# Cached attention for one token: straight-line engine programs become loops, with one place for keys and one for values

## The chip, the core and the metric

The kernel runs on one core of a Trainium2 chip. The core has a tensor engine (PE, whose weight loads the profile lists apart as PEld), a vector engine (DVE), a scalar engine (ACT), a general engine (POOL), a synchronising engine (SP) that issues most of the transfers here, and 16 DMA engines that move the data. All arrays lie in HBM at the start; the working memory on the chip is SBUF, and matrix products land in PSUM. The metric is the device time of one execution in microseconds, lower is better.

## What is computed

One new token `x` of 512 numbers passes two branches whose sums are added to it: attention over a cache of 65,536 keys and values, and a small two-layer network.

```python
def _A_ref(x, k_cache, v_cache, wq, wo):          # 32 query heads, 8 key heads, 128 wide
    q = (x @ wq).reshape(B, Sq, Hq, Dh).transpose(0, 2, 1, 3)
    k = jnp.repeat(k_cache, rep, axis=1)          # rep = 4 query heads share one key head
    v = jnp.repeat(v_cache, rep, axis=1)
    scores = jnp.einsum("bhqd,bhkd->bhqk", q, k) * (Dh ** -0.5)
    p = _softmax(scores, axis=-1)
    o = jnp.einsum("bhqk,bhkd->bhqd", p, v)
    return o.transpose(0, 2, 1, 3).reshape(B, Sq, Hq * Dh) @ wo

def _B_ref(x, w1, w2):
    return jnp.maximum(x @ w1, 0) @ w2            # 512 -> 1792 -> 512

xn = _layernorm(x)
out = x + _A_ref(xn, k_cache, v_cache, wq, wo) + _B_ref(xn, w1, w2)
```

All numbers are float32. Keys and values are 8 heads x 65,536 x 128, so 256 MB each (in units of 1,048,576 bytes); the weights `wq` and `wo` are 8 MB each, `w1` and `w2` 3.5 MB each. Every byte is read once.

## The kernel before

All engine programs are written out in full: the Python loops run when the kernel is built, so that each engine gets one long straight list of instructions. A framework of tiles sets the semaphores between them.

Keys and values come in chunks of 8 MB, four of keys and then four of values for each of the 8 heads (`load_k`, L85, and `load_v`, L94). They go through `ring`, a pool of three equal slots of 64 KB per partition, in the order in which they are used; `wq`, the two weights of the network and `wo` take their turns in the same three slots. SP issues all these loads in one queue and waits before each until the slot that it takes has been read to the end by PE. So up to three loads are under way or waiting to be read at any time.

For a chunk of keys (`score_chunk`) PE makes eight tiles `pt` of scores. A tile is four products (L179) that use 32 columns of PE each, and three buffers of PSUM take turns. DVE transposes each tile in blocks of 32x32 (L184), so that keys lie along partitions, and ACT copies the four useful columns of each block into `scores` (L186), which holds all scores of the head: 512 for each of the four query heads on each partition. After each chunk DVE takes a maximum (L187).

After the four chunks of a head, `softmax` forms the maximum over the whole head: a maximum on DVE (L195), a transpose on PE (L197), a maximum and a scaled diagonal on DVE (L199, L201), a product that hands it to all partitions (L203), a copy (L205), and four exponentials on ACT over 512 elements each (L207), which also sum up. Then, for each chunk of values, `value_chunk` makes 32 products (L218) that add up in `acc_o` over the whole head. `totals` and `output` form the sums and the normalised result of the head, the latter in the middle of the next head's scores. The network's product runs after head 0 (L154, L165, L250). After the last head `wo` is read in six loads (L318, L325), its rows are multiplied as they come in (L250, L265), and the result is added to `x` (L336) and written (L337).

[...] And the order of SP's queue is the order of use: keys of a head, values of that head, keys of the next.

## Time and profile before

| | |
|---|---|
| time, median of 3 runs | 1312.26 us (1312.25 to 1312.28) |
| the profiled execution's own time | 1312.33 us |
| its span, first to last instruction | 1310.6 us |
| moved by DMA | 561.65 MB, mean 429 GB/s |
| PE busy with matmuls | 639.9 us, 4460 records |
| DVE, ACT, POOL busy | 242.7, 103.6 and 0.7 us |
| mean clock granted to PE | 0.73 |

The span leaves out 1.7 us of the execution's time before and after the instructions. Busy time is no time on the path: an engine can be busy half of the time and never be waited for. In a row of a group, the part behind the `|` gives the busy time and the mean ns of one, and then the idle time of that engine just before these instructions with what ended it. In a row of the timeline the first number is the start in us from the begin of the span, the second the length, and the text in brackets the idle time before it.

### The profile page before, as it was taken

To read this page: it belongs to the slowest core of one execution; us is meant where nothing else is said; L and a number is where in the kernel's file an instruction comes from. 1 tells how busy PE (TensorE), PEld (TensorE's weight loads), DVE (VectorE), ACT (ScalarE), POOL (GpSimd) and SP (SyncE) were. 2 spreads that over 40 slices of the span, in tenths; PEclk is the share of its full clock that TensorE was granted. 3 is DMA by queue.
4 is the path that set the end of the run, shared out by engine and by line. 5 is a ranking of instruction groups with operands and counts; after the bars stand their busy time and mean duration, and the time that the engine had idled before them with its cause. 6 is when DMAs were issued, how large, how long until landed. Compare 5 with 4: busy or idle time off the path is not lost.

```text
span 1310.6 us, 10141 instructions
## 1 busy us (share of the span) xinstructions
PE 639.9 (49%) x4460; PEld 166.5 (13%) x4460; DVE 242.7 (19%) x408; ACT 103.6 (8%) x323; POOL 0.7 (0%) x6
## 2 busy tenths in 40 slices
PE   4345354545435544644544543644444563463455
PEld 1011011111111100111111110111111110011111
DVE  2242002230024200422003400233002420032200
ACT  0012000020001200101001110002000120010100
POOL 0000000000000000000000000000000000000000
PEclk9677687677777767767667767777866866776778
DMA  9999999999999999999999999999999999999997
GB/s 416 417 443 423 442 423 438 427 435 441 423 441 427 437 432 433 431 441 419 447 418 443 433 431 435 427 439 423 441 424 441 427 435 433 429 445 428 435 417 313
DMA packets 12428, 561.65 MB, mean 429 GB/s; under 512 B 1368, under 2 KB 1376, under 8 KB 1760
## 3 DMA queue, kind: packets, MB, share of 16 engines
q1 hardware_dynamic: 12240, 561.00, 99.3%
q8 instruction: 35, 0.57, 0.2%
q14 instruction: 9, 0.07, 0.0%
q10 hardware_dynamic: 144, 0.00, 0.0%
HBM read 560.99 MB, written 0.00 MB: 428 GB/s over the span
## 4 chain that ended last, share of the span: by engine, by line
DMA 77%; PE 19%; another core or an unknown queue 3%; ACT 0%; DVE 0%; issue 0%; SPq 0%; DVEq 0%; ACTq 0%
DMA slot<-k 44%; DMA slot<-v 30%; PE pt L179 9%; PE acc_o L218 8%; DMA slot<-wo 3%; PE acc_z L250 1%; ACT scores L207 0%; PE acc_y L265 0%; DVE chunk_max L187 0%; SPq L100 0%; DVE tr L184 0%; DVE z L256 0%; PE pm L203 0%; PE pm L228 0%
## 5 line engine op out<-in xcount | busy, mean ns | idle before, releaser
L179 PE MATMUL pt<-slot,qall 128*32 128x512 f32 x2048 | 295.4, 741 | 314.7 <-DMA slot<-k 314.7
L218 PE MATMUL acc_o<-slot,scores 128*16 128x512 f32 x2048 | 292.1, 734 | 249.3 <-DMA slot<-v 249.3
L184 DVE STREAM_TRANSPOSE tr<-pt 128x512 f32<-128x512 f32 x256 | 183.5, 717 | 829.5 <-PE pt L179 807.1
L186 ACT COPY scores<-tr 128x64 f32<-128x64 f32 x256 | 62.4, 244 | 1094.8 <-DVE tr L184 1094.8
L179 PEld LDWEIGHTS pt<-slot,qall 128*32 128x32 f32 x2048 | 80.7, 133 | 523.2 <-issue 472.5
L218 PEld LDWEIGHTS acc_o<-slot,scores 128*16 128x16 f32 x2048 | 61.4, 113 | 472.2 <-DMA slot<-v 273.6
L207 ACT ACTIVATE scores<-scores,bias 128x512 f32<-128x512 f32 x32 | 37.7, 1179 | 21.1 <-DVE bias L205 21.1
L187 DVE TENSOR_REDUCE chunk_max<-scores 128x4 f32<-128x512 f32 x32 | 33.5, 1047 | 7.7 <-ACT scores L186 7.7
L228 PE MATMUL pm<-part_sum,ones 128*128 128x4 f32 x16 | 4.7, 364 | 42.4 <-ACT scores L207 42.4
L154 PE MATMUL pm<-slot,xn 128*1 128x512 f32 (+1 forms) x96 | 14.7, 752 | 11.1 <-DMA slot<-wq 11.1
L240 DVE COPY o<-acc_o 128x512 f32<-128x512 f32 x8 | 5.3, 657 | 63.2 <-PE acc_o L218 63.2
L243 PE MATMUL pm<-norm,o 128*128 128x4 f32 x64 | 8.5, 257 | 11.2 <-DVE o L240 11.2
L160 DVE TENSOR_SCALAR rows<-pm 128x512 f32<-128x512 f32 x1 | 0.7, 691 | 70.0 <-PE pm L154 70.0
L197 PE MATMUL pm<-ident,m 128*4 128x128 f32 x8 | 2.3, 287 | 19.8 <-DVE m L195 19.8
L243 PEld LDWEIGHTS pm<-norm,o 128*128 128x128 f32 x64 | 7.8, 192 | 19.3 <-DVE o L240 19.3
L230 DVE RECIPROCAL r<-pm 128x4 f32<-128x4 f32 x8 | 1.5, 183 | 45.2 <-PE pm L228 45.2
L250 PE MATMUL acc_z<-slot,oT 128*1 128x512 f32 x48 | 7.3, 770 | 4.7 <-DMA slot<-wo 4.7
L228 PEld LDWEIGHTS pm<-part_sum,ones 128*128 128x128 f32 x16 | 4.0, 310 | 43.1 <-ACT scores L207 43.1
L250 PE MATMUL acc_z<-slot,hT 128*1 128x512 f32 x28 | 6.3, 996 | 2.5 <-DMA slot<-w 2.5
L203 PE MATMUL pm<-dg,ones 4*128 4x4 f32 x16 | 3.6, 296 | 5.0 <-DVE dg L201 5.0
L207 ACT ACTIVATION_READ_ACCUMULATOR scores<-scores,bias 128x1 f32 x32 | 6.0, 186 | 0.0
L154 PEld LDWEIGHTS pm<-slot,xn 128*1 128x1 f32 x96 | 2.8, 99 | 20.9 <-issue 20.6
(56 smaller groups left out, 38.6 us busy)
## 6 DMA issues: line engine op xcount, KB each, us to landing
slot<-wq SPq DMA_DIRECT2D x2, 4096.0 KB, 17.2
slot<-w SPq DMA_DIRECT2D x2, 3584.0 KB, 42.6
slot<-v SPq DMA_DIRECT2D x1, 4096.0 KB, 39.9
slot<-v SPq DMA_DIRECT2D x2, 2048.0 KB, 44.4
slot<-wo SPq DMA_DIRECT2D x1, 4096.0 KB, 41.7
slot<-wo SPq DMA_DIRECT2D x1, 2048.0 KB, 46.2
slot<-wo SPq DMA_DIRECT2D x1, 1024.0 KB, 48.1
slot<-k SPq DMA_DIRECT2D x32, 48.7
```

The costliest lines, as they stand in the source:

```text
L154: nc.tensor.matmul(pr[32 * c : 32 * c + 1, :n], xn[:, a : a + 1], weights(c, a), start=(a == 0), stop=(a == A - 1),)
L179: nc.tensor.matmul(pt[32 * c : 32 * c + 32, :], qall[:, h, :], t[:, lo : lo + TW], start=True, stop=True,)
L184: nc.vector.transpose(tr.rearrange("p b i -> p (b i)"), pt)
L186: nc.scalar.copy(scores[:, b0 : b0 + SUB, :], tr[:, :, :G])
L187: nc.vector.reduce_max(chunk_max[:, :, n], scores[:, n * NB : (n + 1) * NB, :].rearrange("p b g -> p g b"), axis=AX.X,)
L203: nc.tensor.matmul(pb[:, :G], ones[:G, :], dg, start=True, stop=True)
L207: nc.scalar.activation(scores[:, :, g], scores[:, :, g], AF.Exp, bias=bias[:, g : g + 1], scale=scale, accum_out=part_sum[:, g : g + 1],)
L218: nc.tensor.matmul(acc_o[32 * c : 32 * c + WIDE * G, :], scores[:, b : b + WIDE, :].rearrange("p b g -> p (b g)"), t[:, i * 512 : (i + 1) ...
L228: nc.tensor.matmul(pm[:, :G], ones, part_sum, start=True, stop=True)
L240: nc.vector.tensor_copy(o.rearrange("p b d -> p (b d)"), acc_o)
L243: nc.tensor.matmul(pm[:, :G], o[:, b, :], norm[:, b, :], start=(b == 0), stop=(b == WIDE - 1))
L250: nc.tensor.matmul(acc_z[32 * c : 32 * c + 1, :], lhsT, row, start=c not in begun, stop=last)
```

## The change

Each engine gets its own program with its own semaphores, inside one critical section that the framework of tiles does not order. PE, DVE and ACT run hardware loops: PE's body is one part of a head and runs 40 times, the bodies of DVE and ACT are a whole head and run 8 times. SP's and POOL's programs are still written out.

A head is cut into five parts of 7, 7, 6, 6 and 6 tiles (a tile is 2,048 keys, 1 MB), in place of four chunks of eight. For each part its keys and then its values are loaded, in turns, each into one place of its own (`ks`, `vs`, 56 KB per partition). The keys of the next part are issued once DVE has transposed the last tile of this part (`k_free`), the values of the next part once DVE has added this part's products to the sum (`v_free`). PE and DVE always work through seven tiles, also in parts of six; the weights of the seventh are then zero.

The maximum is taken per part, as a running one (`m`), and each part has its own bias. The exponentials are taken straight from the transposed tiles, part by part; ACT's copy of the scores is gone. The products of a part's values add up in `acc_o`, and DVE then forms `acc = alpha * acc + acc_o`, with `alpha` made by ACT from the two biases. At the end of a head DVE corrects the parts' sums and hands both to POOL, which keeps them (`fins`); normalisation is done once, after the last head. The rows of keys and values that are loaded lie 256 KB apart in HBM (64 KB before). The network's weights are loaded and used after the last head, ahead of `wo`, which goes to the place where `wq` was.

```diff
-CHUNK = 16384
+CHUNK = SK
+PART = [7, 7, 6, 6, 6]
+MOST = max(PART)
+NP = len(PART)
+STEPS = HKV * NP
...
-    ring = ctx.enter_context(tc.tile_pool(name="ring", bufs=3))
+    ks = place("ks", MOST * KEYS)
+    vs = place("vs", MOST * KEYS)
+    big = place("big", HKV * 2048)
+    tr = place("tr", MOST * SUB, 32)
+    wt = place("wt", MOST * SUB, G)
...
+        for i in range(STEPS):
+            h, n = divmod(i, NP)
+            lo, nt = sum(PART[:n]), PART[n]
+            src = v[h].rearrange("(p t b) d -> p t (b d)", p=P, b=SUB)[:, lo : lo + nt, :]
+            if i:
+                sy.wait_ge(k_free, i)
+            sy.dma_start(ks[:, : nt * KEYS], k[h, 0, :, lo * KEYS : (lo + nt) * KEYS]).then_inc(k_in, 16)
+            if i:
+                sy.wait_ge(v_free, i)
+            sy.dma_start(vs[:, : nt * KEYS], src.rearrange("p t f -> p (t f)")).then_inc(v_in, 16)
+        sy.wait_ge(k_free, STEPS)
...
+        w1_in = load(sy, "w1_in", t1, w1.rearrange("p a f -> p (a f)"))
+        w2_in = load(sy, "w2_in", t2, w2.rearrange("p j n -> p (j n)"))
...
+        with nc.Fori(0, STEPS, engines=[ENG.PE], head_slot={ENG.PE: 0}):
+            te.wait_ge(k_in, 16).then_inc(k_in, -16)
+            te.wait_ge(q_in, 1).then_inc(q_in, -1)
+            for s in range(MOST):
+                pt = (pa, pb)[s // 2 % 2][:, s % 2, :]
+                for c in range(CT):
+                    at = (s * CT + c) * TW
+                    i = te.matmul(pt[32 * c : 32 * c + 32, :], qcur, ks[:, at : at + TW], start=True, stop=True)
+                    if c == 0 and s in (4, 6):
+                        i._wait_ge(s_dve, s // 2 - 1)
+                if s % 2 or s == MOST - 1:
+                    i.then_inc(s_tiles, 1)
+            te.transpose(pm[:G, :P], m, ident)._wait_ge(s_dve, 3).then_inc(s_max, 1)
+            te.matmul(pm[:, P : P + G], ones[:G, :], dg[:, :G], start=True, stop=True)._wait_ge(s_dve, 4)
+            te.matmul(
+                pm[:, P + G : P + G + 1], rowg, dg[:, G : G + 1], start=True, stop=True
+            ).then_inc(s_max, 1)
+            te.sem_inc(s_dve, -4)
+            te.wait_ge(v_in, 16).then_inc(v_in, -16)
+            te.wait_ge(s_w, 1).then_inc(s_w, -1)
+            n = MOST * SUB // WIDE
+            for i in range(n):
+                c = i % CT
+                mm = te.matmul(
+                    acc_o[32 * c : 32 * c + WIDE * G, :],
+                    wt[:, i * WIDE : (i + 1) * WIDE, :].rearrange("p b g -> p (b g)"),
+                    vs[:, i * 512 : (i + 1) * 512],
+                    start=(i < CT), stop=(i >= n - CT),
+                )
+            mm.then_inc(s_o, 1)
+
+        with nc.Fori(0, HKV, engines=[ENG.DVE], head_slot={ENG.DVE: 0}):
+            for n, nt in enumerate(PART):
+                for s in range(0, MOST, 2):
+                    w = min(2, MOST - s)
+                    i = ve.transpose(
+                        tr[:, s * SUB : (s + w) * SUB, :].rearrange("p b i -> p (b i)"),
+                        (pa, pb)[s // 2 % 2][:, :w, :].rearrange("p i k -> p (i k)"),
+                    )._wait_ge(s_tiles, s // 2 + 1)
+                    if s < 4:
+                        i.then_inc(s_dve, 1)
+                ve.sem_inc(s_tiles, -4)
+                ve.drain().then_inc(k_free, 1)
+                top = m if n == 0 else mc
+                i = ve.reduce_max(top, tr[:, : nt * SUB, :G].rearrange("p b g -> p g b"), axis=AX.X)
+                if n:
+                    ve.drain()
+                    i = ve.tensor_max(m, m, mc)
+                i.then_inc(s_dve, 1)
+                ve.reduce_max(mg, pm[:G, :P], axis=AX.X)._wait_ge(s_max, 1)
+                ve.drain()
+                ve.tensor_scalar(dg, idg, mg, -scale, op0=ALU.mult, op1=ALU.mult).then_inc(s_dve, 1)
+                ve.tensor_copy(bias[:, n, :], pm[:, P : P + G + 1])._wait_ge(s_max, 2).then_inc(s_bias, 1)
...
+                    i = ve.scalar_tensor_tensor(
+                        flat, flat, alpha[:, n : n + 1], acc_o, op0=ALU.mult, op1=ALU.add
+                    )
+                i._wait_ge(s_o, 1).then_inc(v_free, 1)
...
+        with nc.Fori(0, HKV, engines=[ENG.Activation], head_slot={ENG.Activation: 0}):
+            for n, nt in enumerate(PART):
+                se.wait_ge(s_bias, 1).then_inc(s_bias, -1)
+                if n and nt < PART[n - 1]:
+                    b = slice(nt * SUB, PART[n - 1] * SUB)
+                    se.copy(wt[:, b, :].rearrange("p b g -> p (b g)"), zero)
+                for g in range(G):
+                    i = se.activation(
+                        wt[:, : nt * SUB, g], tr[:, : nt * SUB, g], AF.Exp, bias=bias[:, n, g : g + 1],
+                        scale=scale, accum_out=part[:, n, g : g + 1],
+                    )
+                i.then_inc(s_w, 1)
...
```

## The prediction

> **What bounds the kernel now.** I read the page's shares and queues first, then the chain that ended last, then PE's rows in the timeline, because they show when each chunk landed. From the page:

> ```profile
> PE 639.9 (49%) x4460; PEld 166.5 (13%) x4460; DVE 242.7 (19%) x408; ACT 103.6 (8%) x323; POOL 0.7 (0%) x6
> ...
> DMA  9999999999999999999999999999999999999997
> ...
> q1 hardware_dynamic: 12240, 561.00, 99.3%
> q8 instruction: 35, 0.57, 0.2%
> ...
> DMA 77%; PE 19%; another core or an unknown queue 3%; ACT 0%; DVE 0%; issue 0%; SPq 0%; DVEq 0%; ACTq 0%
> ...
> L179 PE MATMUL pt<-slot,qall 128*32 128x512 f32 x2048 | 295.4, 741 | 314.7 <-DMA slot<-k 314.7
> L218 PE MATMUL acc_o<-slot,scores 128*16 128x512 f32 x2048 | 292.1, 734 | 249.3 <-DMA slot<-v 249.3
> ```

> The DMA engines are full in every slice but the last, and PE idles before both kinds of products because data has not landed. PE's 19% of the chain is the time in which a slot is freed while two other loads are still queued. So the kernel is bound by loads; only how well they run, and what lies before the first and behind the last, can move its time.

> How well do they run? PE's rows, the network's weights left out (7/8 of a chunk, after head 0):

> ```profile
> 42.57 9.99 PE L179 MATMUL pt<-slot,qall 128*32 128x512 f32 x64 [12.49 <-DMA slot<-k]
> 63.33 9.85 PE L179 MATMUL pt<-slot,qall 128*32 128x512 f32 x64 [10.77 <-DMA slot<-k]
> 82.69 8.71 PE L179 MATMUL pt<-slot,qall 128*32 128x512 f32 x64 [9.51 <-DMA slot<-k]
> ...
> 332.19 8.53 PE L218 MATMUL acc_o<-slot,scores 128*16 128x512 f32 x64 [9.69 <-DMA slot<-v]
> 352.86 8.44 PE L218 MATMUL acc_o<-slot,scores 128*16 128x512 f32 x64 [12.14 <-DMA slot<-v]
> ...
> 935.46 8.97 PE L218 MATMUL acc_o<-slot,scores 128*16 128x512 f32 x64 [10.95 <-DMA slot<-v]
> 956.10 8.89 PE L218 MATMUL acc_o<-slot,scores 128*16 128x512 f32 x64 [11.67 <-DMA slot<-v]
> ...
> 1287.21 3.36 PE L218 MATMUL acc_o<-slot,scores 128*16 128x512 f32 x16 [3.26 <-DMA slot<-v]
> ```

> The pace is 19.36 us for a chunk of 8 MB (82.69 - 63.33). But some chunks come later: 20.76, 20.67 and 20.64 us at 63.33, 352.86 and 956.10. From the first keys (42.57) to the last piece of values (1287.21) pass 1244.6 us. At the pace, 63 chunks and 7 MB of the network's weights take 63.875 x 19.36 = 1236.6. So **8.0 us are lost** although the engines are never idle. The chain in order of time names what stands there:

> ```profile
> 340.72 12.09 another core or an unknown queue
> ...
> 653.39 10.73 another core or an unknown queue
> 664.12 0.04 issue
> ```

> I read this unknown queue as the instructions' own: 35 fetches of 0.57 MB are 16 KB each, and PE's 4460 matmul records with their 4460 weight loads at 64 bytes each would be 0.57 MB. So PE's long program is read through the same DMA engines while it runs. A fetch holds up one engine of the sixteen, a load lands with its slowest engine, and the late chunks stand some 300 us apart, about eight fetches: the delay shows when an engine is hit again. That is an inference, since the page doesn't name the unknown queue.

> **The change, part by part.** *PE's loop.* A product is two records and two weight loads (4460 of each above); the body has 58 products and a transpose, 234 instructions, 15 KB, run 40 times. If it is fetched once, 35 fetches become some four, for the straight parts at both ends. Gain: up to the 8.0 us; 0 if the cause is another. I take 8.0 and give back 0.6 for the remaining fetches (0 to one late step, 1.3). What is last then is still the load, at its pace.

> [...]

> *Shorter rows.* The loads carry the same bytes in 80 x 128 rows of 56 or 48 KB, before in 64 x 128 rows of 64 KB. What a row costs shows in the second half of `wq`, 4 MB in 512 rows:

> ```profile
> 13.33 5.79 PE L154 MATMUL pm<-slot,xn 128*1 128x512 f32 x32 [8.47 <-DMA slot<-wq]
> ...
> 23.30 5.31 PE L154 MATMUL pm<-slot,xn 128*1 128x512 f32 x32 [2.64 <-DMA slot<-wq]
> ```

> It took 9.97 us, half a chunk in 64 rows 9.68: 0.29 us for 448 rows more. 2,048 rows more cost 1.3 us. A load of 7 tiles takes 16.9 us, one of 6 takes 14.5.

> *One place each for keys and values.* Before, a slot came free with two loads still queued. Now one load runs while the next waits for a flag, so SP's waits matter, and behind them SP's whole queue. Is each flag up in time? Per part, from the start of its scores, with rows around the softmax of one head:

> ```profile
> 1053.26 9.81 PE L179 MATMUL pt<-slot,qall 128*32 128x512 f32 x64 [10.11 <-DMA slot<-k]
> 1059.78 4.15 DVE L184 STREAM_TRANSPOSE tr<-pt 128x512 f32<-128x512 f32 x5 [0.32 <-ACT scores L186]
> 1063.96 0.24 ACT L186 COPY scores<-tr 128x64 f32<-128x64 f32 x1 [0.61 <-DVE tr L184]
> 1064.24 1.05 DVE L187 TENSOR_REDUCE chunk_max<-scores 128x4 f32<-128x512 f32 x1 [0.31 <-ACT scores L186]
> 1065.32 0.17 DVE L195 TENSOR_REDUCE m<-chunk_max 128x4 f32<-128x16 f32 x1
> 1066.47 0.59 PE L203 MATMUL pm<-dg,ones 4*128 4x4 f32 x2 [0.62 <-DVE dg L201]
> 1067.35 1.19 ACT L207 ACTIVATE scores<-scores,bias 128x512 f32<-128x512 f32 x1 [3.14 <-DVE bias L205]
> ```

> and, from the page's groups and the list of DMA issues, the nearest rows for the sum on DVE and for a load on an idle queue:

> ```profile
> L240 DVE COPY o<-acc_o 128x512 f32<-128x512 f32 x8 | 5.3, 657 | 63.2 <-PE acc_o L218 63.2
> xT<-x ACTq DMA_DIRECT2D x1, 2.0 KB, 1.8
> ```

> Scores: 7/8 of a chunk's 8.4 to 10.0 us, so 7.4 to 8.7, mean 8.1 (295.4 / 32 x 7/8). The last transpose ends 0.86 behind PE (1063.93 against 1063.07); with a drain 1.0. From there to the first exponential 3.42 us, less the copy's 0.31, plus a maximum against the running one (0.17) and a second small product (0.6); three drains, which no row shows, I put at 0.25 (0 to the 0.17 of the shortest DVE row each). That is 4.1. An exponential is over 96 or 112 elements; between the copy of 64 (0.24) and 512 (1.19) that is about 0.35, with its sum 0.45: four take 1.8 (1.0 to 4.7). So the weights stand at 8.1 + 1.0 + 4.1 + 1.8 = 15.0 us, the values of a 6-tile part at 14.5. The 56 records of value products take another 8.0 (292.1 / 32 x 7/8; 7.4 to 8.7), the sum on DVE 0.7 to 0.8, and the flag, SP's issue and its way at most the 1.8 of a whole 2 KB load.

> - Keys: wanted at 8.1 + 1.0 + 1.8 = 10.9 us, due at 14.5 when the values have landed. Margin 3.6.
> - Values: wanted at 15.0 + 8.0 + 0.8 + 1.8 = 25.6, due when the next keys have landed, 29.0 for two loads of 6 tiles. Margin 3.4; with the slow end of both products 2.1.

> So no load starts late, and I cost these waits at nothing; their cover is the margin. Behind a missed margin PE, DVE and ACT all wait. POOL's copies of the query and the results fall into the same gaps, once per head. The network's two loads move from behind head 0 to the end of SP's queue, behind the last keys' flag (same margin as keys); their bytes cost the same there.

> *Work that leaves or grows off the path.* ACT's 256 copies go (62.4 us busy by their group); the padded seventh tile adds 24 tiles and 96 value products, some 9% of PE's 587 us, all below a load's time. Price 0 while the margins hold.

> *Begin.* SP passes the entry of a critical section before its first load, which now starts at 0.73 us: 0.3 (0 to 0.5).

> *End.* After the last values come 7 MB and 8 MB of weights, 17 + 20 us, in which PE must do the value products (8), DVE the head's end (about 3), the network (two groups of 5 to 6.3 us and their copies, 13) and the normalisation (3): 27 us, as the first 4 MB of `wo` land (17 + 10). From there on the order is as before:

> ```profile
> 1297.16 7.30 PE L250 MATMUL acc_z<-slot,oT 128*1 128x512 f32 x48 [4.74 <-DMA slot<-wo]
> 1305.50 2.13 PE L265 MATMUL acc_y<-slot,oT 128*1 128x128 f32 x64
> ```

> PE then needs 10.5 us, all but the last of them beside the loads. The cover is just long enough: 0.5 us (0 to 4).

> **The sum**, against the profiled execution of 1312.33 us: its span of 1310.6 - 8.0 + 0.6 + 1.3 + 0.3 + 0.5 = 1305.3; with the 1.7 us outside the span 1307.0. The median before is 1312.26, 0.07 less than the profiled one, which I neglect. Forecast: 0.4% faster, 1304.5 to 1309.6 in its own case. A change of 0.2%, 2.6 us, is about what can be told from none.

> **The rivals.**

> 1. *The fetches stay.* If PE reads its body again at each of 40 turns, or the 8.0 us have another cause, the gain is missing: 1312.3 + 1.3 + 0.8, and 1.1 for five more fetches, gives 1314 to 1316, no change or slightly slower. Against it: the body is smaller than one fetch. For it: no row shows a loop. It decides from some 25 fetches on.
> 2. *A part's chain outlasts two loads* (slower): the values' flag comes behind the keys. Two short steps per head, parts 2 to 3 and 3 to 4; a late start of the first gives the second as much room, so each us over 29.0 costs about 8 us in all. From 3.4 us longer than built it starts, from 0.7 us beyond that it eats the gain. Unseen drains, flags on sequencers and reads of `tr` at a stride of 128 bytes speak for it. With 1.5 us over: 1319.
> 3. *Rows 256 KB apart load slower* (slower). The pace per byte is the same in `wq` (rows 8 KB apart) as in chunks (64 KB apart) but for the price per row, so nothing points to it; 256 KB is not in the trace. Each 1% of the 1240 us of keys and values is 12.4 us: 1319 at 1%. It decides from 0.4% on. [...]
> 4. *The end isn't covered:* 4 us more, 1311, no change.

> **How the numbers follow.** Forecast 0.62, rival 1 0.12, rival 2 0.08, rival 3 0.10, rival 4 0.08. Faster by over 0.2%: nine tenths of the forecast, 0.57. Within: rival 4, half of rival 1, the rest of the forecast, 0.16. Slower: rivals 2 and 3, half of 1, 0.27 with what I have not thought of. The range runs from the forecast's low end to 1321, which takes in rivals 1 and 4 and the milder halves of 2 and 3.

> **What would show it.** Right: under ten instruction fetches in the queues' part; parts of 7 and 6 tiles landing 33.9 and 29.0 us behind one another without late steps; PE's idle time before scores ended by DMA of keys; SP waiting for PE or DVE, with DMA full all the same. Wrong: 40 fetches or more; DMA digits below 9 within the parts; loads of 6 tiles that take over 14.6 us; PE's last records far behind the last load.

## The result, and the profile after

The changed kernel takes 1310.09 us (median of 22 runs, 1308.58 to 1312.99) against 1312.32 us (22 runs, 1312.09 to 1313.01) for the kernel before on the same chip: a ratio of 0.9984, with a 95% interval of 0.9978 to 0.9991. It is 0.16% faster, where 0.4% was forecast, and its median lies above the 1304.5 to 1309.6 us of the forecast's own case. Its runs spread over 4.4 us where those before spread over 0.9. The profiled execution is its fastest, 1308.58 us with a span of 1306.8.

The page of the kernel after, shares and queues:

```profile
PE 748.4 (57%) x4958; PEld 214.8 (16%) x4958; DVE 294.9 (23%) x474; ACT 88.3 (7%) x372; POOL 4.6 (0%) x22
...
DMA  9999999999999999999999999999999999999998
...
q1 hardware_dynamic: 14248, 561.00, 99.6%
q8 instruction: 3, 0.05, 0.0%
q14 instruction: 5, 0.04, 0.0%
```

Queue 8 carries PE's instructions, as the run with PE's loop written out shows below: its 35 fetches have become 3. The DMA engines are still full. Queue 14, also of instructions, holds five of 8 KB, nine before. The waits of SP's queue, with the total, the number and the longest, show the new order of things:

```profile
SPq L158 <- DVEq L343: 632.4, 39, 49.0
SPq L161 <- DVE acc L360: 454.0, 31, 16.4
```

SP now waits for DVE before each load, and only one load is queued behind the running one. One part in the timeline of after, one of those whose flags came last, from the start of its scores to the issue of the next values:

```profile
573.48 3.64 PE L307 MATMUL pa<-ks,qcur 128*32 128x512 f32 x16 [6.70 <-PEq L302]
...
582.97 0.67 DVE L336 STREAM_TRANSPOSE tr<-pb 128x512 f32<-128x512 f32 x1
583.70 0.33 SPq L158 DMA_DIRECT2D ks<-k  x1
...
588.93 8.21 PE L323 MATMUL acc_o<-vs,wt 128*16 128x512 f32 x56 [2.48 <-PEq L319]
597.21 0.75 DVE L360 SCALAR_TENSOR_TENSOR acc<-acc,alpha,acc_o 128x512 f32<-128x512 f32 x1 [10.55 <-PE acc_o L323]
597.98 0.33 SPq L161 DMA_DIRECT2D vs<-v  x1
```

The keys' issue stands 10.2 us behind the first scores, the products with the values 15.5, the values' issue 24.5. And PE's rows at both ends, from the first scores to the last values, with the row of SP that writes the result:

```profile
13.62 6.55 PE L242 MATMUL pa<-big,xn 128*1 128x512 f32 x32 [8.16 <-DMA big<-wq]
...
23.57 5.00 PE L242 MATMUL pa<-big,xn 128*1 128x512 f32 x32 [1.84 <-DMA big<-wq]
42.73 3.64 PE L307 MATMUL pa<-ks,qcur 128*32 128x512 f32 x16 [12.61 <-PEq L302]
59.70 8.29 PE L323 MATMUL acc_o<-vs,wt 128*16 128x512 f32 x56 [4.64 <-PEq L319]
...
1266.09 7.55 PE L323 MATMUL acc_o<-vs,wt 128*16 128x512 f32 x56 [2.34 <-PEq L319]
...
1303.82 0.66 SPq L142 DMA_DIRECT2D y<-x  x1
```

The first of these products start within 0.3 us of their load's landing, so the rows tell when that was. At the old pace of 19.36 us for 8 MB a load of 7 MB takes 16.94 and one of 6 MB 14.52. Behind the first keys come 31 of the former and 48 of the latter, 1222.1 us; from 42.73 to 1266.09 pass 1223.4. So the loads of keys and values run at their pace to 1.3 us, where the kernel before lost 8.0. But the first keys land 19.2 us behind the second half of `wq`, 2.2 more than a load of 7 MB takes. In the kernel before they landed on time (19.3 us for 8 MB).

### The profile page after: what moved, and what is told of

Same layout as the page of the kernel before. It is cut to its first block, busy times and chain, and to the rows that moved or that the text cites. A ratio compares the mean times of both kernels' runs of the same rounds, so it can differ in the third digit from the quotient of the medians.

```text
span 1306.8 us, 11612 instructions
## 1 busy us (share of the span) xinstructions
PE 748.4 (57%) x4958; PEld 214.8 (16%) x4958; DVE 294.9 (23%) x474; ACT 88.3 (7%) x372; POOL 4.6 (0%) x22
## 3 DMA queue, kind: packets, MB, share of 16 engines
q1 hardware_dynamic: 14248, 561.00, 99.6%
## 5 line engine op out<-in xcount | busy, mean ns | idle before, releaser
L323 PE MATMUL acc_o<-vs,wt 128*16 128x512 f32 x2240 | 328.5, 750 | 128.6 <-PEq L319 128.6
L307 PE MATMUL pa<-ks,qcur 128*32 128x512 f32 x1280 | 220.1, 820 | 285.8 <-PEq L302 285.8
L336 DVE STREAM_TRANSPOSE tr<-pa 128x1024 f32<-128x1024 f32 x80 | 100.0, 1250 | 404.2 <-PE pa L307 404.2
L307 PE MATMUL pb<-ks,qcur 128*32 128x512 f32 x960 | 139.3, 685 | 0.0
L323 PEld LDWEIGHTS acc_o<-vs,wt 128*16 128x16 f32 x2240 | 76.4, 114 | 347.2 <-issue 347.2
L384 ACT ACTIVATE wt<-tr,bias 128x96 f32<-128x96 f32 (+1 forms) x160 | 73.1, 465 | 875.5 <-ACTq L379 875.5
L307 PEld LDWEIGHTS pa<-ks,qcur 128*32 128x32 f32 x1280 | 48.6, 134 | 420.0 <-issue 409.1
L336 DVE STREAM_TRANSPOSE tr<-pb 128x1024 f32<-128x1024 f32 x80 | 76.9, 962 | 38.0 <-PE pb L307 38.0
L307 PEld LDWEIGHTS pb<-ks,qcur 128*32 128x32 f32 x960 | 41.2, 138 | 110.5 <-issue 86.6
L384 ACT ACTIVATION_READ_ACCUMULATOR wt<-tr,bias 128x1 f32 x160 | 29.9, 187 | 0.0
L345 DVE TENSOR_REDUCE mc<-tr 128x4 f32<-128x384 f32 (+1 forms) x32 | 26.2, 819 | 3.7
```

Of the source, the lines that this page charges most:

```text
L307: i = te.matmul(pt[32 * c : 32 * c + 32, :], qcur, ks[:, at : at + TW], start=True, stop=True)
L323: mm = te.matmul(acc_o[32 * c : 32 * c + WIDE * G, :], wt[:, i * WIDE : (i + 1) * WIDE, :].rearrange("p b g -> p (b g)"), vs[:, i * 512 : ...
L336: i = ve.transpose(tr[:, s * SUB : (s + w) * SUB, :].rearrange("p b i -> p (b i)"), (pa, pb)[s // 2 % 2][:, :w, :].rearrange("p i k -> p ( ...
L345: i = ve.reduce_max(top, tr[:, : nt * SUB, :G].rearrange("p b g -> p g b"), axis=AX.X)
L384: i = se.activation(wt[:, : nt * SUB, g], tr[:, : nt * SUB, g], AF.Exp, bias=bias[:, n, g : g + 1], scale=scale, accum_out=part[:, n, g : ...
```

## The experiments

The question is where the other 3 us of the forecast went, and why the runs spread. The kernel before was run beside each group, each on another chip: 1312.25 us (first four), 1312.42 (next four) and 1312.3 (last four). So groups can be compared to some 0.2 us. Where a single load or fetch has a time below, it comes from the trace's records of single transfers: a load lands with its last piece, and it is late by what it takes beyond the pace (beyond 9.9 us for the first 4 MB of `wo`, whose rows are short).

**The changed kernel again.**

> The changed kernel once more, beside the three that follow, to see its spread and a second profiled execution. Its runs so far spread over 4.4 us (1308.6 to 1313.0), those of the kernel before over 0.9. Theory A (a flag that comes late now and then): 1309.5 to 1311, and in the profiled execution the loads of 6 tiles do not all stand 14.5 us apart: some start late, and the time over 1308.6 is made of such steps. Theory B (rows 256 KB apart load unevenly): the same time, but the late steps come where the next load had been issued well ahead. Theory C (fetches of instructions): the late steps stand at the few fetches alone, at the begin and the end.

Measured 1310.23 us (11 runs, 1308.44 to 1312.69), ratio 0.9983 (0.9974 to 0.9992). This profile's span is 1308.4, 1.6 more than that of the first one, and its rows tell where:

```profile
13.54 6.39 PE L242 MATMUL pa<-big,xn 128*1 128x512 f32 x32 [8.06 <-DMA big<-wq]
...
23.48 6.54 PE L242 MATMUL pa<-big,xn 128*1 128x512 f32 x32 [2.00 <-DMA big<-wq]
42.54 3.64 PE L307 MATMUL pa<-ks,qcur 128*32 128x512 f32 x16 [10.96 <-PEq L302]
...
1265.94 9.12 PE L323 MATMUL acc_o<-vs,wt 128*16 128x512 f32 x56 [2.41 <-PEq L319]
...
1305.48 0.66 SPq L142 DMA_DIRECT2D y<-x  x1
```

The last values land 0.15 us earlier than in the first profile and the result is written 1.66 us later. So this difference lies behind the last values. The network's two weights, in the first profile:

```profile
ks<-w SPq DMA_DIRECT2D x2, 3584.0 KB, 17.7
```

and in this one:

```profile
ks<-w SPq DMA_DIRECT2D x2, 3584.0 KB, 18.6
```

The second of them lands at 1284.24 us, 1.6 late. A fetch for PE begins at 1282.10, while that load runs. In the first profile the same fetch begins at 1287.81, in the load behind it, which is 0.2 late.

**PE's loop written out.** The parts stay as they are; only PE's program is long again.

```diff
-        with nc.Fori(0, STEPS, engines=[ENG.PE], head_slot={ENG.PE: 0}):
+        for _ in range(STEPS):
```

> The changed kernel with PE's loop alone undone: its 40 turns are written out, all other engines keep their loops, loads and flags as they are. If the fetches of PE's program are what cost the kernel before its 8.0 us, some 40 fetches come back and the time rises by 6 to 9 us over the changed kernel beside it: 1316 to 1319, slower than the kernel before. If the late chunks of the kernel before had another cause, the time stays at 1310, with 40 fetches in the queue. Should the loads' flags be late anyway, the fetches cost more than 8 us, since the one load ahead covers less than the three slots did: up to 1325.

Measured 1316.93 us (6 runs, 1316.16 to 1319.78), ratio 1.0038 (1.0025 to 1.005). Its queue of PE's instructions, and PE's first rows:

```profile
q8 instruction: 39, 0.64, 0.2%
```

```profile
23.39 5.31 PE L242 MATMUL pa<-big,xn 128*1 128x512 f32 x32 [2.98 <-DMA big<-wq]
42.37 3.64 PE L307 MATMUL pa<-ks,qcur 128*32 128x512 f32 x16 [12.13 <-PEq L302]
```

36 fetches more than in the changed kernel cost 6.7 us. They are 0.59 MB more (0.64 against 0.05) for 39 turns more, 15 KB a turn, the size that the prediction gave the body from an assumed 64 bytes for each instruction. With nothing else changed, this is the loop's whole worth, and the prediction's reading of the late chunks holds. The records agree: the three late chunks that the prediction names in the kernel before each have a fetch for PE under way (at 46.68, 341.14 and 944.40 us). Each of that kernel's 35 fetches is one packet of 16 KB, which takes 1.0 to 1.3 us. Many loads with a fetch are on time, though, in both kernels, and the latest ones that have one here lose 1.4 us. So a fetch cost up to some 1.4 us here, or nothing.

The first keys are late here too, 19.0 us behind `wq`, 2.0 more than the pace, and PE's fetch comes only behind them, at 45.87. What falls into their load is four fetches of queue 14.

**Half of the score products.** The tiles of scores are also set to zero at the start.

```diff
...
-                for c in range(CT):
+                for c in range(CT // 2):
                     at = (s * CT + c) * TW
```

> The changed kernel with two of the four score products of a tile left out (the other half of the scores is stale, so the output isn't the reference's). PE's scores take about 4 us instead of 8, so both flags of a part come 3 to 4 us sooner; loads, rows and loops are the same. Theory A (late flags): the spread shrinks to under 1 us and the median falls to 1308.0 to 1308.6. Theory B (rows 256 KB apart) and theory C (fetches): the time and the spread stay as in the changed kernel beside it, 1309.5 to 1311.

Measured 1310.09 us (11 runs, 1308.77 to 1314.9), ratio 0.9989 (0.998 to 0.9998). The run seems to speak against late flags, but its edit did not do what it was for. Groups of this kernel:

```profile
L307 PE MATMUL pa<-ks,qcur 128*32 128x512 f32 x640 | 218.4, 817 | 285.7 <-PEq L302 285.7
L307 PE MATMUL pb<-ks,qcur 128*32 128x512 f32 x480 | 137.9, 682 | 0.0
```

and of the changed kernel:

```profile
L307 PE MATMUL pa<-ks,qcur 128*32 128x512 f32 x1280 | 220.1, 820 | 285.8 <-PEq L302 285.8
...
L307 PE MATMUL pb<-ks,qcur 128*32 128x512 f32 x960 | 139.3, 685 | 0.0
```

Half of the products keep PE busy for the same time: a tile's four products, each on its own 32 columns, ran side by side, and their records overlap (1280 records of 820 ns in 220 us). The chain was not shortened: the values are issued 24.1 us behind the first scores here and in the changed kernel (median of the parts of six tiles). So the run decides nothing about the flags.

**Parts that lie together in HBM.** Each part is one block in memory, so rows are 48 or 56 KB apart, not 256.

```diff
...
-            src = v[h].rearrange("(p t b) d -> p t (b d)", p=P, b=SUB)[:, lo : lo + nt, :]
+            src = v[h, lo * KEYS * P : (lo + nt) * KEYS * P].rearrange("(p f) -> p f", p=P)
```

The keys are cut in the same way, and both arrays are laid out like this beforehand.

> The changed kernel with the keys and values of each part laid out one behind the other in HBM, so that the 128 rows of a load lie 56 or 48 KB apart instead of 256 KB. Rows, loads, flags and loops are the same. Theory B (rows 256 KB apart load slower or unevenly): the median falls by 1.5 us or more and the spread shrinks. Theories A and C: no change, 1309.5 to 1311.

Measured 1309.56 us (9 runs, 1307.58 to 1309.85), ratio 0.9977 (0.9967 to 0.9986). The interval overlaps with that of the changed kernel, so no gain is shown; the spread is narrower.

**Less work at the end, and both together.** The rows of head 6 of `wo` go the cheaper way (`acc_z`), so PE's program behind the loop is shorter.

```diff
-DIRECT = 6
+DIRECT = 7
```

> The changed kernel with one number changed: DIRECT 7 instead of 6, so that the rows of head 6 are multiplied like those of heads 0 to 5, and PE's straight part behind the loop has 12 products, 48 instructions, fewer. In the changed kernel two fetches for PE stand in the last 25 us, the last one among the last small loads, and in one of its profiled executions the last load landed 2.4 us behind the one before, 0.7 without it. Theory C (the few remaining fetches make the rest of the gap to the forecast): one fetch fewer, the last load 0.7 us behind the one before, the time 0.5 to 1.7 us below the changed kernel's 1310.2. If the end is bound by PE's work instead: no gain or up to 1 us slower, since the sum over the heads is copied later.

> Both edits that may gain: parts one behind the other in HBM, and the 12 products fewer behind the loop. The contiguous parts alone gave 1309.56 with no run above 1309.9, where the changed kernel has a quarter of its runs above 1310.8. Theory B (rows 256 KB apart cause the slow runs): again no run above 1310. Theory C: 0.5 to 1.7 us below the contiguous parts alone, 1308 to 1309. If the slow runs come back, the tight spread of the contiguous parts was chance.

Measured 1310.58 us (11 runs, 1309.7 to 1311.27), ratio 0.9986 (0.9977 to 0.9995), and for both edits 1310.39 (11 runs, 1308.99 to 1312.64), ratio 0.9986 (0.9977 to 0.9995). With both edits the spread is back, so the narrow one of the run with contiguous parts was most likely chance, and the distance of the rows does not explain it. The two fetches behind the loop stayed, so this edit says nothing of their price.

**Exponentials made twice.** A second set of the four exponentials of each part, into a spare place.

```diff
...
+                for g in range(G):
+                    i = se.activation(
+                        spare[:, : nt * SUB, g], tr[:, : nt * SUB, g], AF.Exp, bias=bias[:, n, g : g + 1],
+                        scale=scale, accum_out=spart[:, n, g : g + 1],
+                    )
...
```

> The changed kernel with the four exponentials of a part made once more, into places that nobody reads, ahead of the real ones: ACT's stretch between the maximum and the value products grows by 1.8 us in every part, all else is the same. By the prediction's margin of 3.4 us for the values' flag nothing moves: 1310. By the profiled execution the margin is smaller, about 1.4 us against the slowest DMA engine and none against the fastest: then values of parts 2 to 3 and 3 to 4 start late and the time rises by 2 to 8 us.

Measured 1328.33 us (4 runs, 1326.26 to 1335.21), ratio 1.0132 (1.0106 to 1.0158): 18 us for some 2 us more in each part's chain. A margin of 3.4 us would have hidden them. From issue to landing, in this kernel:

```profile
ks<-k SPq DMA_DIRECT2D x24, 6144.0 KB, 20.1
vs<-v SPq DMA_DIRECT2D x24, 6144.0 KB, 19.4
```

and in the changed kernel:

```profile
ks<-k SPq DMA_DIRECT2D x24, 6144.0 KB, 19.8
vs<-v SPq DMA_DIRECT2D x24, 6144.0 KB, 19.4
```

The medians are alike, but they hide what differs. In the first profile of the changed kernel each of the 24 value loads of six tiles is issued 4.2 us or more ahead of the landing before it, and lands on time. Here twelve of the 24 are late, by 0.2 to 3.0 us: they were issued some 2 to 5 us ahead and took 18.2 to 19.7 us from issue to landing (median 19.1), where the load itself takes 14.5. Others were on time, one of them issued only 2.5 us ahead. The late loads needed 3.6 to 5.2 us beside their own time. How late the values' flag comes is seen in the 23 parts of six tiles that have a part behind them: in the changed kernel their issue lies 23.0 to 24.5 us behind the first scores, median 24.1; with the exponentials made twice the median is 26.2. The changed kernel stands just ahead of the edge: of its loads behind the first two only one is over 0.2 us late in either profile, by 0.3 and 0.4.

**Five parts in PE's loop.** The body is a whole head, five times 15 KB, in 8 turns.

```diff
-        with nc.Fori(0, STEPS, engines=[ENG.PE], head_slot={ENG.PE: 0}):
+        with nc.Fori(0, HKV, engines=[ENG.PE], head_slot={ENG.PE: 0}):
+            for _ in range(NP):
```

> The changed kernel with PE's body five parts long, 8 turns instead of 40; the same instructions run in the same order. The body is five times some 245 instructions, about 78 KB. If PE keeps a body of that size, the fetches stay under ten and the time is the changed kernel's, 1310. If only a body within one fetch of 16 KB stays, each turn fetches it again: some 40 fetches and 1316 to 1318, as with the loop written out.

Measured 1310.22 us (median of 10 runs, nine from 1309.76 to 1312.89 and one of 1337.77); the ratio of the nine is 0.9985 (0.9976 to 0.9995). There are 7 fetches:

```profile
q8 instruction: 7, 0.11, 0.0%
```

Four more than with one part, and none for the seven later turns (the first five begin between 33 and 172 us, the last two behind the loop): this body of 75 KB was not fetched again.

**Three places.** Loads take three places of 56 KB by turns; `wq` begins in the second and third, and the last weights take the places as they come free. PE's body is three parts. A load is issued when the load three before it has been read, so two loads can be queued behind one that is being read. The 15 MB of weights behind the keys and values move to these places as well. The kernel before, too, had three places.

```diff
-    ks = place("ks", MOST * KEYS)
-    vs = place("vs", MOST * KEYS)
-    big = place("big", HKV * 2048)
+    slots = [place(n, MOST * KEYS) for n in ("s0", "s1", "s2")]
...
+            dst = slots[j % 3][:, : nt * KEYS]
+            if j % 2 == 0:
+                if i > 1:
+                    sy.wait_ge(v_free, i - 1)
...
+            else:
+                if i:
+                    sy.wait_ge(k_free, i)
...
+        with nc.Fori(0, STEPS // 3, engines=[ENG.PE], head_slot={ENG.PE: 0}):
+            for p in range(3):
+                one_part(2 * p % 3, (2 * p + 1) % 3)
```

> Keys and values take three places of 56 KB by turns; PE's body is three parts, 13 turns and one part written out behind them. Each load now has a whole load's time more until its place must be free. Theory 'too little room' (the values' flag comes 0 to 0.4 us before it is needed, so any hitch of a DMA engine makes a load start late, and the next one too): the late starts of 0.5 to 0.8 us go, the time is 1309 to 1309.8 and the runs lie within 1 us of one another, as those of the kernel before do. Rival 'the spread has another cause': time and spread stay as in the changed kernel, 1308.5 to 1313. Two or three more fetches than in the changed kernel cost 0 to 1 us in both.

Measured 1307.69 us (5 runs, 1307.28 to 1308.33), ratio 0.9965 (0.9952 to 0.9979): 2.4 us less than the changed kernel, and all its runs lie below every run of that kernel. From its list of DMA issues, its queues, and PE's rows:

```profile
q8 instruction: 6, 0.10, 0.0%
...
s<-k SPq DMA_DIRECT2D x24, 6144.0 KB, 34.5
s<-v SPq DMA_DIRECT2D x24, 6144.0 KB, 34.2
```

```profile
42.62 3.64 PE L326 MATMUL pa<-s,qcur 128*32 128x512 f32 x16 [11.03 <-PEq L321]
...
1265.52 7.64 PE L342 MATMUL acc_o<-s,wt 128*16 128x512 f32 x56 [2.34 <-PEq L338]
...
1302.85 0.66 SPq L141 DMA_DIRECT2D y<-x  x1
```

A load is now issued 34 us before it lands, a whole load earlier. From the first scores to the last values pass 1222.9 us, 0.5 less than in the changed kernel, and from the last values to the issue of the result 37.3 us, where the two profiles of the changed kernel have 37.7 and 39.5. So the keys and values gain 0.5 us by the room, and the end is shorter by 0.4 to 2.2, although three more fetches are made. Behind the last values a fetch for PE falls into a load here too (at 1287.65), and that load is on time.

**Three places, exponentials made twice.**

> The kernel with three places, with the four exponentials of a part made once more (their results are not used), some 2.5 us more in each part's chain. With two places this cost 18 us. Theory 'it was the values' flag': with a load's time more of room nothing is late, within 1 us of the kernel with three places. Rival 'the exponentials cost by themselves (a busier engine, more reading of SBUF)': 10 us or more again.

Measured 1309.48 us (11 runs, 1307.94 to 1310.0), ratio 0.9977 (0.9968 to 0.9986): 1.8 us more than with three places alone, where the same edit cost 18 with two. So the 18 us were the values' flag. What is left lies at the end, where nothing hides the last part's chain. PE's rows there:

```profile
1293.97 6.80 PE L443 MATMUL acc_z<-s,oT 128*1 128x512 f32 x48 [0.28 <-DVE oT L472]
...
1301.89 1.93 PE L494 MATMUL acc_y<-s,oT 128*1 128x128 f32 x64
```

and with three places alone:

```profile
1292.10 7.03 PE L436 MATMUL acc_z<-s,oT 128*1 128x512 f32 x48 [0.69 <-DMA s<-wo]
...
1300.24 2.15 PE L487 MATMUL acc_y<-s,oT 128*1 128x128 f32 x64
```

The products with `wo` wait for `oT`, the result of the chain, and no longer for the load, and the last ones start 1.65 us later.

**No alignment of the loops.** Without it the loops' first instructions follow what stands before them.

```diff
-        with nc.Fori(0, STEPS, engines=[ENG.PE], head_slot={ENG.PE: 0}):
+        with nc.Fori(0, STEPS, engines=[ENG.PE]):
```

The loops of DVE and ACT are changed alike.

> The changed kernel without the alignment of the loops' first instruction to the start of a fetched block, in all three engines. The first keys and values land 2.1 us later than at the pace, beside fetches of PE, DVE and ACT at the loops' entry. Theory 'the entry's fetches cost it': DVE's and ACT's bodies then mostly lie in what is already read, two to four fetches fewer, 1308 to 1309. Rival 'these loads are late for another reason, or the fetches stay where a body crosses a block': 1309.5 to 1310.5; a body of PE that is read again at each turn would show as 40 fetches and 6 to 7 us more.

> Three places and no alignment together. If both theories hold, 1307.5 to 1309 with a spread under 1 us; if only one, as that kernel alone; if neither, 1310 as the changed kernel.

Measured 1308.74 us (7 runs, 1307.73 to 1309.88), ratio 0.9971 (0.9959 to 0.9982), and with three places 1307.36 us (5 runs, 1307.0 to 1307.72), ratio 0.9963 (0.9949 to 0.9977). The latter has the lowest median of all, by 0.3 us, which is within the intervals. With two places and no alignment, the second queue of instructions and PE's first rows:

```profile
q14 instruction: 3, 0.02, 0.0%
```

```profile
23.39 3.61 PE L242 MATMUL pa<-big,xn 128*1 128x512 f32 x32 [2.49 <-DMA big<-wq]
40.52 3.64 PE L307 MATMUL pa<-ks,qcur 128*32 128x512 f32 x16 [11.97 <-PEq L302]
58.89 7.95 PE L323 MATMUL acc_o<-vs,wt 128*16 128x512 f32 x56 [5.68 <-PEq L319]
```

The first keys are on time now, 17.1 us behind `wq`, but the first values take 18.4, 1.4 too many. Together 35.5 us, against 36.1 in the changed kernel and 33.9 at the pace. No fetch falls into the load of the first keys any more; that of PE's body begins at 46.04, in the load of the first values, and that load is the late one. So here the lateness went where the fetches went. That two places gain 1.35 us by it and three places only 0.3 is within the intervals.

## Why the prediction was right in part and wrong in part

*The fetches of PE's long program: right.* The term was -8.0 with 0.6 given back, 7.4 together. That a looped body is fetched once was an assumption, which nothing before the result showed; the changed kernel has 3 fetches in place of 35. Undoing the loop alone gives 6.7 us for 36 fetches.

*What remains of the fetches: this is the step that failed, by its size.* The 0.6 was "0 to one late step, 1.3", for PE alone. The step overlooked that PE, DVE and ACT all enter their loops while the first keys are under way (four fetches begin between 35.25 and 41.16 us in the first profile) and that PE fetches again behind the last values (at 1287.81 and 1301.16). The first keys land 2.2 us late (19.2 against 16.9). The runs show that this is the fetches' doing: with PE's loop written out the four fetches of queue 14 fall into that load, PE's does not, and it is 2.0 late; without alignment none falls into it and it is on time. That queue 14 is DVE's and ACT's is an inference. Behind the last values another 0.2 us is lost in the first profile and 1.6 in the second.

*Shorter rows: too dear.* Forecast +1.3. A load of 6 MB lands 14.5 us behind the one before, which is the pace of the long rows. With three places all the loads behind the first keys together lose 0.8 us (1222.9 against 1222.1), so 2,048 more rows cost at most that.

*Begin: right.* The first products start at 13.62 in place of 13.33, 0.3 us later. The 0.3 was my estimate; SP's first load is issued at 0.96 us, 0.73 before.

*One place each: the margin was mis-sized, but as built it cost little.* The chain itself was forecast well: keys' flag at 9.1 us (8.1 + 1.0; median 9.4), the products with the values at 14.5 to 15.0 (14.8), values' issue at 23.3 to 23.8 (24.1). What failed is "the flag, SP's issue and its way at most the 1.8 of a whole 2 KB load". Loads that came too late needed 3.6 to 5.2 us between issue and landing beside their 14.5, at least twice that bound. Due at 29.0 and issued by this chain at 15.0 + 8.0 + 0.8 = 23.8, the values then have a margin of 0 to 1.6 us, not 3.4. Two runs show it: 18 us for 2.1 us more of the chain, and 1.8 for the same with a third place. So rival 2, which I let begin 3.4 us further on, stood close by; its price of some 8 us for each us over the margin was not too high (18 for at most 2.1). In the kernel as built these waits cost little: the loads of keys and values take 0.5 us more than with three places. That they did not cost more is luck, since the cover was nearly gone.

*The sum again*, against the span before, from the rows of the two profiles of the changed kernel (first, second): begin +0.3, +0.2; first keys +2.3, +2.2; the loads of keys and values behind them -6.8, -6.7 (8.0 lost before, 1.3 now); behind the last values, beyond the 15 MB at the pace, +0.4, +2.1. That is -3.8 and -2.2. The second profile's time, 1310.23 us, is near the median; the first is the fastest run. Forecast was -5.3. The keys and values came out at the forecast's -6.7 (-8.0 and 1.3 for rows), which is luck in part: rows cost less and late flags more. What is missing is 1.6 us at the first keys, beyond the 0.6, and up to 1.6 at the end, beyond the 0.5.

*The end: within its bounds, but above its middle.* It was +0.5, 0 to 4; measured are +0.4 and +2.1. So rival 4 came true in part in the second profile. My reading is that a fetch behind the loop costs its 1.3 us or nothing, as it hits a DMA engine that is behind the others or ahead. The records bear it out: in all ten profiles with two places the latest of the loads behind the last values, 0.2 to 1.6 us late, is one that a fetch for PE falls into. In the second profile the first and the last of the 16 DMA engines finish 1.2 us apart before that load and 2.8 after it. With three places the engines finish 2.0 to 2.4 us apart, and in three profiles the fetch costs nothing. But no run took these fetches away, so it is not proved, and why the runs spread over 4.4 us with two places and 1.0 with three stays open: a late load of 1.6 can be only a part of it. A third place makes the kernel 2.4 us faster; by the profiles 0.5 of it is the room for keys and values, and the rest lies at the end.

*Rival 1* fell (3 fetches), *rival 3* too: loads land at the old pace, and with the rows together the time is the same within the intervals. Rows 256 KB apart loaded here like rows 64 KB apart: 6 MB take 14.5 us, as at the old pace (14.52).

## What to carry to other kernels

## What the runs showed that was not expected

- Halving the score products, each on 32 columns, did not change PE's busy time (220.1 us for 1280 records, 218.4 for 640), so these products ran side by side.
- A loop's body of 75 KB on PE was fetched once for its 8 turns (7 fetches in all).
- A load that a fetch of 16 KB fell into was up to 1.6 us late, or on time.
- The same kernel with one load queued spreads over 4.4 us (22 runs), with two over 1.0 (5 runs; 0.7 without alignment, 5 runs; 2.1 with the exponentials made twice, 11 runs).
